# Later value, maxima and transposition transfers, more places for turned terms and remainder rows, and x pairs in middle beats, in a gated attention and feed-forward kernel

## Chip, cores and metric

One core of one Trainium2 chip. The time is the device time of one execution in microseconds (us): the kernel before takes 1727.56 us as the median of 3 runs (1726.11 to 1729.72). TensorE is called PE here, VectorE DVE, ScalarE ACT, GpSimd POOL. SyncE is called SP; its queue issues all the transfers of this kernel.

## The reference, cut to what matters

```
def reference(A_x, A_wq, A_wk, A_wv, A_wo, A_beta, B_x, w_gate, w_up, w_down, gate_w):
    g = sigmoid((x * gate_w).sum(-1, keepdims=True))
    a = A_ref(x, wq, wk, wv, wo, beta)
    b = (silu(x @ w_gate) * (x @ w_up)) @ w_down
    return g * a + (1 - g) * b

    # A_ref: 32 heads of 18, N = 4 segments s of L = 512 rows
    logits = qs @ ks.T * scale + mask          # inside one segment
    a_dot = softmax(logits) @ vs
    a_mem = (phi(qs) @ M) / (phi(qs) @ z + 1e-6)
    o = sigmoid(beta) * a_mem + (1 - sigmoid(beta)) * a_dot
    M, z = M + phi(ks).T @ vs, z + phi(ks).sum(0)
```

x has 2048 rows of 576, w_gate and w_up are 576 x 4608, w_down is 4608 x 576, all float32.

## The kernel before, in words

Three stages follow one another, and the matrix work of all of them is on PE.

**Stage 1** (to about 234 us) makes q, k, v and the memory terms, and leaves them in DRAM for what follows: `stk` and `stw` (stacked queries and keys), `vd` (values), `med` (memory). Its last loop, `for n in range(8)` over units of `v`, also starts what the next stage needs first: raw weights, splits of x and the first remainder rows.

**Stage 2** (234 to about 1640 us) is the feed-forward part, with the attention of all heads woven into it. `seq` lists 72 positions: two halves of the rows (`half`) times 36 column blocks of 128 (`f`). A position makes gate and up of one block for 1024 rows with seven products instead of eight, `seven(bank, j)` for j = 0 to 6. One product is six matmuls (L1392) of 128x512 on split float16 weights `wo__` and x tiles `xo`, and a seventh (L1395) that carries the columns of x that are left over from 512; its weights are the remainder rows `rem`, a tile `rh` that `r_fetch(f)` loads from DRAM (`rc`). There are two such tiles, `rhs[f % 2]`. Between products the position calls `tick()` eight times, k = 0 to 7 (5 and 6 with no product between them), and each tick ends in `beat(k, half)`.

A beat does three things in this order, all of it issued in program order on the engines:

1. it runs the deferred work that is due (`due`, filled by `defer(beats, fn)`): splits of weights, loads, sums, the splits `hh` and `hl` of the hidden block (ACT L1261, DVE L1264);
2. it runs some of the sixteen down-projection groups. They exist in every third position (`q == 0`), cover the three blocks before, and are nine matmuls each (L1161, weights `hh` and `hl`, moving side `dw`). Two banks of PSUM take turns for them, and DVE frees a bank by adding it into `ya` (L1168 the first time, L1170 after that). How many groups a beat gets is in `SHARE`, and for position 3 alone in `FSHARE`, chosen by `early[0]`;
3. it runs attention steps (`next(att)`), by a credit that grows by `TICK`. In the first half steps run only in positions with groups, in beats 2 to 7.

The attention generator `att_gen` counts steps `tau`; five steps are one unit `u` of 4 heads by 512 rows, `n` the step in it. One step touches several units, each at another age: scores for the row maxima (`s_bank`, PE L890, DVE L908), the maxima transposed, stored to DRAM by `m_store` (L982) and read back as an extra row of the queries by `row_load` (L301), then twelve steps after the first the transposed scores with their exponentials (`t_bank`: PE L1001, ACT L1005, POOL L1013), two steps later the float16 split of the terms (DVE L1101 or ACT L1103, POOL L1105) and three steps after that the products with the values (`pv_step`, L1029 and L1031). `v_fetch` loads the values of the next 20 steps from `vd`. In the second half, even units are "turned": exponentials of untransposed scores (L942), split (POOL L947), transposed by DMA (`turn`, L951), then multiplied (`pv_turned`, L963). The parts for turned units sit in `homes`, six places for each name, and `TURN` lists how many steps after `tau` each part runs.

Between the halves stands a break of `BREAK` = 10 beats that runs the last sixteen groups of the first half: beats 0 and 1 are called as ordinary beats, and as `brk[0]` is set there they also run an attention step each; the other eight run two groups each, in four banks.

The first half makes its weight tiles from raw weights (`w_make`: POOL L370, ACT L374, DVE L378) and keeps them in DRAM (`wc`), the second loads them back. `x_second` makes the seven combinations of x for the second half in positions 24 to 35: POOL `total` (L1311), ACT `high` (L1318), DVE `low` (L1321). Its table `steps` gives for each the position after 24 + 6z, the beat, the function and the combination j.

**Stage 3** (from about 1640 us) is the output projection; its weights are split by `c_open` once attention has run out (DVE L1209).

Of the kernel before, what the change touches and what calls it, by code (L numbers as in the profile page):

```python
# [42 lines left out]
TURN = (1, 3, 7, 17)  # L43
# [5 lines left out]
FSHARE = (0, 0, 0, 2, 3, 4, 4, 3)  # L49
# [21 lines left out]
def gated_mix(ctx, tc, xT, xrest, wf, wfr, wfh, wd, wv, wo, beta, cmask, ident, bmask, out):  # L71
# [283 lines left out]
    def r_fetch(f):  # L355
        nc.sync.dma_start(rhs[f % 2][:96].rearrange("p j n -> p (j n)"), rc[f // 4, :, f % 4])
# [38 lines left out]
    with ExitStack() as st:  # L395
# [337 lines left out]
        for s in range(NSEG):  # L733
# [49 lines left out]
            if s == 3:  # L783
# [12 lines left out]
                for z in range(2):  # L796
                    rhs.append(wop.tile([P, 7, P], F16, name=f"rh{z}", bufs=1))
                start = w_make(0)
            for n in range(8):
# [23 lines left out]
                else:  # L823
# [4 lines left out]
                    for k, t, v in ((0, rhs[0][96:], 0.0), (1, kst[0], -1.0), (3, kst[1], -1.0), (6, rhs[1][96:], 0.0)):  # L828
                        if n == k:
                            nc.gpsimd.memset(t, v)  # L830
                    if n == 1:
                        r_fetch(0)
# [11 lines left out]
    with ExitStack() as st:  # L844
# [76 lines left out]
        turned = set()  # L921

        def turn_open(u):
# [5 lines left out]
            for name, ids in (("pq", ((2, 0), (2, 1), (3, 0))), ("pk", ((3, 1), (4, 0), (4, 1)))):  # L929
                homes[name] = []  # L930
                for a, b in ids:
                    t = xo.tile([P, 2, 8 * P], F16, name=f"xo{a}{b}")
                    homes[name] += [t[:, z] for z in range(2)]

        def spot(name, u, n):
            return homes[name][(5 * (u // 2) + n) % 6]
# [113 lines left out]
        def att_gen():  # L1050
            N = 10 * NB
            for tau in range(N + TL + VL + 5):
# [15 lines left out]
                z = tau - TL - VL - 1  # L1068
# [186 lines left out]
        opened, early, brk = [0], [0], [0]  # L1255
# [14 lines left out]
        def beat(k=None, half=0):  # L1270
# [8 lines left out]
            share = (SHARE, FSHARE)[early[0]][k]  # L1279
            for n in range(max(share, 1)):  # L1280
# [4 lines left out]
                credit[0] += TICK[half][busy] * (opened[0] if half else k > 1 or brk[0])  # L1285
# [8 lines left out]
        def x_second(new, z):  # L1294
# [105 lines left out]
        for pos, (half, f) in enumerate(seq):  # L1400
# [68 lines left out]
            early[0] = int(pos == CH)  # L1469
            turn_of[0] = () if pos < 24 else (1, 3)  # L1470
            ops, rem = wops.pop((half, f)), rhs[f % 2]
# [41 lines left out]
            if f == FT - 1:  # L1513
                groups += feed(half, f)
                if half == 0:
                    brk[0] = 1
# [109 lines left out]
```

## Time and profile before

| what | us |
| --- | --- |
| median of 3 runs | 1727.56 |
| the profiled execution's own time | 1725.81 |
| its span, first to last instruction | 1724.1 |
| stage 1, 0 to 234: PE busy | 227.39 |
| second stage, 926 to 1640 (second half): PE busy of 714 | 705.65 |
| stage 3, 1640 to 1724: PE busy | 80.67 |
| DVE busy, whole span | 1347.3 |
| ACT busy, whole span | 1066.3 |
| POOL busy, whole span | 885.6 |

A timeline row reads: start, duration, engine, line, operation, output<-inputs, shape, and in brackets how long the engine sat idle before it and what ended that idle time. A row of waits reads: who waited for whom, then us in total, how often, and the longest. A row of windows gives start and end, the length, and for each engine the busy time with the number of instructions, then the granted PE clock (1.00 is full), the busy share of the DMA engines, and GB/s. A row of the chain of waits gives start, length, and the work or transfer that the end hung on.

### The profile page before, as it was taken

Reading aid. Unit: us, or ns where it says so; the run is one execution under the profiler, and the core shown is the slowest. Engines: PE = TensorE matmul, PEld = TensorE weight load, DVE = VectorE, ACT = ScalarE, POOL = GpSimd, SP = SyncE. Lnnn points to the kernel's source line nnn. Section 1 sums busy time; section 2 is a strip of 40 time slices with the busy share of each in tenths; the row PEclk is TensorE's granted clock in tenths of the full one; section 3 lists DMA queues with packets and bytes.
Section 4 is the critical chain, followed back from the end, with each engine's and each line's share of the span. In section 5 each row is a group of like instructions: output and inputs, shape, how many; then the busy total and the mean of one; then the engine's idle time right before and its main releaser. Section 6 shows DMA issues by size and latency. Waiting matters only on the chain.

```text
span 1724.1 us, 35228 instructions
## 1 busy us (share of the span) xinstructions
PE 1684.5 (98%) x12267; PEld 1093.1 (63%) x12267; DVE 1347.3 (78%) x3286; ACT 1066.3 (62%) x1907; POOL 885.6 (51%) x1187
## 2 busy tenths in 40 slices
PE   9999998999999999999999999999999999999999
PEld 7898865556655665565555556656656655665599
DVE  6687666789888988888886888887878787875555
ACT  6666567677777777766774664665565566464411
POOL 3336552266656665565553755555555555543121
PEclk9999999999999999999999999999999999999999
DMA  8666675665776666536435476786587669653543
GB/s 282 219 229 221 221 257 203 206 210 169 239 229 198 184 220 194 171 112 193 158 124 172 118 173 154 164 196 146 132 203 174 129 166 203 155 122 115 183 142 137
DMA packets 341670, 311.30 MB, mean 181 GB/s; under 512 B 193396, under 2 KB 258676, under 8 KB 341492
## 3 DMA queue, kind: packets, MB, share of 16 engines
q1 hardware_dynamic: 341492, 309.05, 61.8%
q8 instruction: 96, 1.57, 0.4%
q14 instruction: 82, 0.67, 0.1%
HBM read 183.20 MB, written 99.55 MB: 164 GB/s over the span
## 4 chain that ended last, share of the span: by engine, by line
PE 71%; DVE 10%; ACT 9%; issue 3%; DMA 3%; POOL 2%; SPq 1%; DVEq 0%; ACTq 0%; POOLq 0%
PE bank L1392 30%; PE bank L1161 19%; PE bank L224 7%; PE bank L1395 5%; PE bank L890 3%; PE bank L1001 2%; PE bank L1029 1%; ACT L1499 1%; DVE ya L1170 1%; ACT row L1499 1%; ACT pe L1005 1%; PE bank L1031 1%; PE bank L963 1%; DVE junk L908 1%; DMA stw<-q 1%
## 5 line engine op out<-in xcount | busy, mean ns | idle before, releaser
L1161 PE MATMUL bank<-dw,hh 128*128 128x320 f16 (+1 forms) x2304 | 437.9, 287 | 13.8 <-DVE ya L1170 9.5
L1161 PE MATMUL bank<-dw,hl 128*128 128x320 f16 (+1 forms) x1152 | 330.5, 287 | 0.9 <-DVE dw L1141 0.6
L1105 POOL TENSOR_TENSOR p<-pe,p 128x512 f16<-128x512 f32 x220 | 271.7, 1235 | 78.7 <-DVE p L1101 50.2
L1161 PEld LDWEIGHTS <-hh 128*128 128x128 f16 x2304 | 224.9, 98 | 100.9 <-issue 19.9
L1005 ACT ACTIVATE pe<-bank 128x512 f32<-128x512 f32 x220 | 130.1, 591 | 190.6 <-PE bank L1001 181.9
L1170 DVE SCALAR_TENSOR_TENSOR ya<-bank,sc,ya 128x320 f32<-128x320 f32 x352 | 177.2, 511 | 57.2 <-PE bank L1161 55.0
L1395 PE MATMUL bank<-xr,rh 128*128 128x512 f16 x504 | 191.2, 379 | 1.9 <-DMA rh<-rc 1.9
L908 DVE CUSTOM_DVE_ANT_0 junk<-bank,cm 128x128 bf16<-128x128 f32 (+2 forms) x352 | 169.3, 481 | 14.0 <-PE bank L890 7.4
L1013 POOL TENSOR_SCALAR_AFFINE_SELECT pe<-pe 128x256 f32<-128x256 f32 (+1 forms) x220 | 89.5, 407 | 164.6 <-ACT pe L1005 153.0
L1264 DVE SCALAR_TENSOR_TENSOR hl<-hh,row 128x512 f16<-128x512 f16 x144 | 125.2, 870 | 47.8 <-ACT hh L1261 46.7
L1161 PEld LDWEIGHTS <-hl 128*128 128x128 f16 x1152 | 112.7, 98 | 30.2 <-DVE hl L1264 0.6
L890 PE MATMUL bank<-kst,qst 108*128 108x512 bf16 (+3 forms) x512 | 124.8, 299 | 5.9 <-ACT pe L1005 5.2
L1001 PE MATMUL bank<-qst,kst 111*128 111x512 bf16 (+3 forms) x352 | 103.3, 300 | 3.9 <-ACT pe L1005 2.8
L1101 DVE CAST p<-pe 128x512 f16<-128x512 f32 x202 | 106.4, 527 | 0.0
L1497 DVE TENSOR_TENSOR row<-bank,row 128x512 f32<-128x512 f32 x72 | 49.7, 690 | 64.4 <-ACT bank L1496 64.4
L370 POOL TENSOR_TENSOR ws<-raw 128x256 f32<-128x256 f32 x72 | 66.5, 924 | 64.2 <-DMA raw<-in_wf_dram 35.3
L224 PE MATMUL bank<-xo,qhi 128*128 128x512 f32 x288 | 93.0, 403 | 0.5 <-DVE xo L134 0.2
L1261 ACT ACTIVATE hh<-row 128x512 f16<-128x512 f32 x144 | 89.0, 618 | 3.8 <-DVE row L1507 3.8
L467 POOL TENSOR_TENSOR q<-qr,q 128x512 bf16<-128x512 f32 x36 | 47.8, 1328 | 84.3 <-ACT q L466 74.8
L1492 ACT ACTIVATE row<-bank 128x512 f32<-128x512 f32 x72 | 42.9, 596 | 76.4 <-PE bank L1395 76.2
L1395 PEld LDWEIGHTS <-rh 128*128 128x128 f16 x504 | 49.3, 98 | 61.8 <-issue 2.4
L1496 ACT ACTIVATE bank<-bank 128x512 f32<-128x512 f32 x72 | 41.9, 582 | 72.6 <-PE bank L1395 70.7
(1090 smaller groups left out, 4228.3 us busy)
## 6 DMA issues: line engine op xcount, KB each, us to landing
xo<-in_wf_dram SPq DMA_DIRECT2D x65, 320.0 KB
raw<-in_wf_dram SPq DMA_DIRECT2D x72, 256.0 KB
dc<-dw SPq DMA_DIRECT2D x36, 432.0 KB
dw<-dc SPq DMA_DIRECT2D x36, 432.0 KB
rh<-rc SPq DMA_DIRECT2D x72, 168.0 KB
draw<-in_wd_dram SPq DMA_DIRECT2D x36, 288.0 KB
xo<-in_xT_dram SPq DMA_DIRECT2D x33, 256.0 KB
vd<-vps SPq DMA_DIRECT2D x8, 912.0 KB
```

The lines of the kernel that those rows point to most:

```text
L224: nc.tensor.matmul(t, st[n], mv[n], start=(n == 0), stop=(n == 13))
L890: nc.tensor.matmul(t[:, c:c + w], qs[:KR, pr, P * i:P * i + P], ks[:KR, pr, 0:w], start=True, stop=True)
L908: nc.vector.tensor_tensor_reduce(junk.bitcast(BF)[:, :w], t[:, c:c + w], cm[:, L - w:L], 1.0, -3.0e38, OP.add, OP.max, m[:, k:k + 1])
L1001: nc.tensor.matmul(t[:, c:c + w], ks[:KR + 3, pr, P * j:P * j + P], qs[:KR + 3, pr, P * j:L], start=True, stop=True)
L1005: nc.scalar.activation(pe, t, AF.Exp, scale=SCALE)
L1101: nc.vector.tensor_copy(p1, pe)
L1105: nc.gpsimd.tensor_sub(p2, pe, p1)
L1161: nc.tensor.matmul(t, p, d[:, q, cs], start=(f == CH * c and n == 0), stop=(f == CH * c + CH - 1 and n == 2))
L1170: nc.vector.scalar_tensor_tensor(ya[:, i, cs], t, inv[c], ya[:, i, cs], op0=OP.mult, op1=OP.add)
L1264: nc.vector.scalar_tensor_tensor(lo, hi, -STEP, src, op0=OP.mult, op1=OP.add)
L1392: nc.tensor.matmul(t, w[:, p, z], x[z][:, q], start=first and n == 0, stop=False, skip_group_check=True)
L1395: nc.tensor.matmul(t, rem[:, RPOS[j]], XR[j], start=False, stop=True, skip_group_check=True)
```

## The change

The edits, in the order of the program:

- the remainder rows get a third tile: `rhs[f % 3]`. The load for block 1 moves into the last loop of stage 1, and the planned one at position 0 is left out. The third tile's rest is cleared on POOL two beats into stage 2 (one instruction more);
- position 3 takes its groups by `SHARE` like all others; `FSHARE` and `early` are gone;
- `brk` is gone: beats 0 and 1 of the break run no attention steps, so that all attention steps from there on come two later against the positions and beats. There are 340 steps as before;
- in `att_gen`, the maxima are stored and read back one step later in their unit (`m_store` at n = 2, `row_load` at n = 4), the values are fetched five steps later, and the DMA transposition of a turned term one step later (`TURN[2]` 7 to 8). The turned low and high terms `pk` get four more places in a pool of their own (ten in all);
- in `x_second` the sums and splits named in the diff move to beats 4 and 5 from beats 5 to 7.

```diff
-TURN = (1, 3, 7, 17)
+TURN = (1, 3, 8, 17)
-FSHARE = (0, 0, 0, 2, 3, 4, 4, 3)
...
-        nc.sync.dma_start(rhs[f % 2][:96].rearrange("p j n -> p (j n)"), rc[f // 4, :, f % 4])
+        nc.sync.dma_start(rhs[f % 3][:96].rearrange("p j n -> p (j n)"), rc[f // 4, :, f % 4])
...
-                for z in range(2):
+                for z in range(3):
                     rhs.append(wop.tile([P, 7, P], F16, name=f"rh{z}", bufs=1))
...
-                    if n == 1:
-                        r_fetch(0)
+                    if n in (1, 5):
+                        r_fetch(n // 5)
...
+        tp = pool(st, "tp", 1)
...
+            homes["pk"] += [tp.tile([P, 8 * P], F16, name=f"pk{z}") for z in range(4)]
         def spot(name, u, n):
-            return homes[name][(5 * (u // 2) + n) % 6]
+            return homes[name][(5 * (u // 2) + n) % len(homes[name])]
...
-                if n == 1 and 1 <= u <= 2 * NB and u - 1 not in turned:
+                if n == 2 and 1 <= u <= 2 * NB and u - 1 not in turned:
                     m_store(u - 1)
-                if n == 3 and 1 <= u <= 2 * NB and u - 1 not in turned:
+                if n == 4 and 1 <= u <= 2 * NB and u - 1 not in turned:
                     row_load(u - 1)
...
-                z = tau - TL - VL - 1
+                z = tau - TL - VL - 6
                 if z % 20 == 0 and 0 <= z < N and z // 20 + 1 < 4 * NSEG:
                     v_fetch(z // 20 + 1)
...
+        defer(2, lambda: nc.gpsimd.memset(rhs[2][96:], 0.0))
...
-            share = (SHARE, FSHARE)[early[0]][k]
+            share = SHARE[k]
...
-                credit[0] += TICK[half][busy] * (opened[0] if half else k > 1 or brk[0])
+                credit[0] += TICK[half][busy] * (opened[0] if half else k > 1)
...
-                steps += ((0, 3, high, 0), (0, 4, low, 0), (0, 5, total, 1), (0, 5, high, 5), (0, 6, low, 5), (0, 7, total, 4),
+                steps += ((0, 3, high, 0), (0, 4, low, 0), (0, 4, total, 1), (0, 4, high, 5), (0, 5, low, 5), (0, 5, total, 4),
...
-                steps += ((0, 5, high, 0), (0, 6, low, 0), (0, 7, total, 1), (1, 2, high, 5), (1, 3, low, 5), (1, 4, total, 4),
+                steps += ((0, 4, high, 0), (0, 5, low, 0), (0, 5, total, 1), (1, 2, high, 5), (1, 3, low, 5), (1, 4, total, 4),
...
-                plan.append((1 if nxt[1] else 10, lambda f=nxt[1]: r_fetch(f)))
+                if pos:
+                    plan.append((1 if nxt[1] else 10, lambda f=nxt[1]: r_fetch(f)))
...
-            ops, rem = wops.pop((half, f)), rhs[f % 2]
+            ops, rem = wops.pop((half, f)), rhs[f % 3]
```

Three places show how the instructions move. The first is PE in position 3, from the end of its third product (`xr` are the leftover columns of x, `rh` the remainder rows; `hh` are weights of a down group). Before:

```order
L1395 MATMUL bank_3113<-xr_1449,rh_2445 128x512
L1392 LDWEIGHTS wo__3051
L1392 MATMUL bank_3115<-xo_2260,wo__3051 128x512
L1392 LDWEIGHTS wo__3051
L1392 MATMUL bank_3115<-xo_2260,wo__3051 128x512
```

and now:

```order
L1397 MATMUL bank_3118<-xr_1449,rh_2444 128x512
L1162 LDWEIGHTS hh
L1162 MATMUL bank_3181<-dw,hh 128x320
L1162 LDWEIGHTS hh
L1162 MATMUL bank_3181<-dw,hh 128x320
L1162 LDWEIGHTS hl
L1162 MATMUL bank_3181<-dw,hl 128x320
```

Two down groups, 18 matmuls, come before the fourth product instead of after it, two after that product as before, and beats 5 and 6 run one group less each.

The second is PE at the break, from the last product of position 35 (`qst` and `kst` are attention's stacked queries and keys, `p` its terms). Before:

```order
L1395 MATMUL bank_11838<-xr_1756,rh_2445 128x512
L1001 LDWEIGHTS kst_2766
L1001 MATMUL bank_11873<-qst_2768,kst_2766 128x384
L890 LDWEIGHTS qst_2436
L890 MATMUL bank_11875<-kst_2437,qst_2436 128x256
L1001 LDWEIGHTS kst_2766
L1001 MATMUL bank_11873<-qst_2768,kst_2766 128x128
L890 LDWEIGHTS qst_2436
L890 MATMUL bank_11875<-kst_2437,qst_2436 128x256
L1029 LDWEIGHTS p_11461
L1029 MATMUL bank_11898<-v,p_11461 128x57
```

and now:

```order
L1397 MATMUL bank_11842<-xr_1756,rh_2446 128x512
L1162 LDWEIGHTS hh
L1162 MATMUL bank_11884<-dw,hh 128x320
L1162 LDWEIGHTS hh
L1162 MATMUL bank_11884<-dw,hh 128x320
L1162 LDWEIGHTS hl
L1162 MATMUL bank_11884<-dw,hl 128x320
```

Two attention steps went from between the last product and the down groups into the second half.

The third is DVE in position 24, around one `low` of `x_second` (`xo`<-`xo`,`sc`). Before:

```order
L1101 CAST p_9063<-pe 128x512
L378 SCALAR_TENSOR_TENSOR wo__8895<-ws,sc,wo__8895 128x512
L1321 SCALAR_TENSOR_TENSOR xo_8702<-xo_8702,sc 128x512
L1170 SCALAR_TENSOR_TENSOR ya<-bank_9071,sc,ya 128x320
L974 TENSOR_REDUCE acc<-bank_9082 128x152
```

and now:

```order
L377 SCALAR_TENSOR_TENSOR wo__8804<-raw,sc,wo__8804 128x512
L1323 SCALAR_TENSOR_TENSOR xo_8706<-xo_8706,sc 128x512
L1171 SCALAR_TENSOR_TENSOR ya<-bank_8999,sc,ya 128x256
L1171 SCALAR_TENSOR_TENSOR ya<-bank_9010,sc,ya 128x320
L907 ISA junk,mb_2438<-bank_9027,cm 128x128
```

The low stands one beat earlier, behind the split of another pair of weights (L377), and the addition into `ya` that was behind it is now behind a cast and a split alone.

More of the change, by code (lines that the diff above doesn't have):

```diff
@@ L827, in gated_mix @@
                         first_split(6, n)
-                    for k, t, v in ((0, rhs[0][96:], 0.0), (1, kst[0], -1.0), (3, kst[1], -1.0), (6, rhs[1][96:], 0.0)):
+                    for k, t, v in ((0, rhs[0][96:], 0.0), (1, kst[0], -1.0), (3, kst[1], -1.0), (4, rhs[1][96:], 0.0)):
                         if n == k:
                             nc.gpsimd.memset(t, v)
-                    if n == 1:
-                        r_fetch(0)
+                    if n in (1, 5):
+                        r_fetch(n // 5)
                     if n > 2:
@@ L1254, in gated_mix @@
         credit = [-1.0]
-        opened, early, brk = [0], [0], [0]
+        opened = [0]
         later = [False]
@@ L1468, in gated_mix @@
             later[0] = half == 1 and f > 0
-            early[0] = int(pos == CH)
             turn_of[0] = () if pos < 24 else (1, 3)
-            ops, rem = wops.pop((half, f)), rhs[f % 2]
+            ops, rem = wops.pop((half, f)), rhs[f % 3]
             hh = fp.tile([P, 2, L], F16, name="hh")
@@ L1515, in gated_mix @@
                 if half == 0:
-                    brk[0] = 1
                     for n in range(BREAK):
```

## The prediction

> **What bounds the kernel now.** I read the page's busy times first, then the windows by stage, then who waited for whom on PE, then the timeline and the chain of waits at the long stalls.
>
> ```profile
> PE 1684.5 (98%) x12267; PEld 1093.1 (63%) x12267; DVE 1347.3 (78%) x3286; ACT 1066.3 (62%) x1907; POOL 885.6 (51%) x1187
> ```
>
> PE is busy for 98% of the span, and its work is the same before and after. So the change can only win from PE's idle time and from stretches at a lower clock. The windows say where those lie:
>
> ```profile
> 234.00:300.00 66.00, 58.50 (x312) 30.65 (x311) 41.05 (x93) 48.79 (x91) 20.63 (x33) 0.97 0.68 235
> 825.00:926.00 101.00, 97.53 (x686) 58.55 (x684) 84.59 (x170) 66.63 (x113) 48.20 (x53) 0.98 0.45 152
> 926.00:1640.00 714.00, 705.65 (x5723) 424.28 (x5722) 550.89 (x1476) 408.31 (x681) 378.23 (x498) 1.00 0.64 159
> 280.00:290.00 10.00, 6.46 (x34) 3.68 (x33) 4.57 (x13) 6.75 (x14) 0.00 (x0) 0.83 0.98 375
> 905.00:915.00 10.00, 9.32 (x61) 6.62 (x61) 7.18 (x19) 4.30 (x8) 7.04 (x7) 0.83 0.60 206
> ```
>
> The first five positions and the break hold the only two places in the feed-forward stage with a clock of 0.83; one such window of ten costs 10 x 0.17 = 1.7 us of matmul progress. The second half has 714.00 - 705.65 = 8.35 us of idle time in 714, in small pieces. The waits on PE:
>
> ```profile
> PE bank L1161 <- DVE ya L1170: 9.5, 16, 1.6
> PE bank L890 <- ACT pe L1005: 5.2, 11, 0.8
> PE bank L1161 <- DVE ya L1168: 3.8, 3, 2.8
> PE bank L1001 <- ACT pe L1005: 2.8, 1, 2.8
> PE bank L1395 <- DMA rh<-rc: 1.9, 1, 1.9
> PE bank L1001 <- DMA wo__12361<-wc: 1.1, 1, 1.1
> ```
>
> These six rows are 24.3 us, and the change touches the owner of each: places, order, or step.
>
> **Part A, remainder rows.** Position 1 waits for its remainder rows, which were issued in position 0 behind other transfers:
>
> ```profile
> 242.83 4.62 DMA rh<-rc
> 247.59 0.38 PE L1395 MATMUL bank<-xr,rh 128*128 128x512 f16 x1 [1.93 <-DMA rh<-rc]
> 253.00 0.72 POOL L370 TENSOR_TENSOR ws<-raw 128x256 f32<-128x256 f32 x1 [7.34 <-DMA raw<-in_wf_dram]
> ```
>
> The third tile lets this load go out in stage 1, so the 1.93 us stall has no cause left. The one POOL clear that is added (two beats into stage 2) falls into the 7.34 us in which POOL sat waiting. That same row is also what can eat the gain: the next weights are made from raw data that lands at 253.00 whenever PE arrives, so a PE that is 1.93 us early may wait for weights instead. Bounds 0 and 1.93; I take the middle, 1.0.
>
> **Part B, position 3.**
>
> ```profile
> 273.25 1.46 PE L1392 MATMUL bank<-xo,wo__3051 128*128 128x512 f16 x6
> 276.79 0.30 PE L1161 MATMUL bank<-dw,hl 128*128 128x320 f16 x1 [0.59 <-DVE dw L1141]
> 281.98 0.38 PE L1161 MATMUL bank<-dw,hh 128*128 128x256 f16 x2 [0.74 <-DVE ya L1168]
> 276.77 6.58 DMA xo<-in_wf_dram
> 285.93 0.69 PE L1161 MATMUL bank<-dw,hh 128*128 128x320 f16 x2 [2.80 <-DVE ya L1168]
> 303.66 2.21 PE bank L1161 x18
> ```
>
> Here 0.59 + 0.74 + 2.80 = 4.13 us are idle, and behind the 2.80 the clock falls (the window at 280), another 1.7. The cause of the 2.80 is a chain: a transfer lands 6.58 us after its issue, ACT waits for it, DVE behind ACT, and the eviction of a down bank behind that, so PE has nothing it may do. Now two groups (2.21 us for 18 matmuls) stand ahead of the fourth product. That work sits earlier, and what PE still owes at 285.93 is 2.21 less. Against it: the earlier pair starts at 273.25 and reaches its last factor 14 matmuls later, 273.25 + 14 x 2.21/18 = 274.97, while that factor is only there at 276.79. So 1.82 us of stall stand where 0.59 stood, 1.23 more, before later stalls shrink by it. What comes out: if the transfer's chain still decides at 285.93, the PE work after it is 2.21 shorter and the clock loss may stay; that is 2.2. If the 2.80 goes with its clock loss, 2.80 + 1.7 - 1.23 = 3.3, and with the 0.74 and the rest of the 0.59 it could be 4.4. If the stall at the front drops the clock instead, a loss of 1.6. I take 2.5, nearer the first; bounds -1.6 and 4.4.
>
> **Part C, x pairs.** Twice a down group waits 1.58 us because the split of an x pair stands ahead of the addition into `ya`:
>
> ```profile
> 690.90 0.55 DVE L1170 SCALAR_TENSOR_TENSOR ya<-bank,sc,ya 128x320 f32<-128x320 f32 x1 [0.39 <-PE bank L1161]
> 696.83 1.65 DVE L1321 SCALAR_TENSOR_TENSOR xo<-xo,sc 128x512 f16<-128x512 f32 x1
> 698.99 0.43 PE L1161 MATMUL bank<-dw,hh 128*128 128x320 f16 x2 [1.58 <-DVE ya L1170]
> 815.23 0.43 PE L1161 MATMUL bank<-dw,hh 128*128 128x320 f16 x2 [1.58 <-DVE ya L1170]
> 683.92 0.74 DVE L1321 SCALAR_TENSOR_TENSOR xo<-xo,sc 128x512 f16<-128x512 f32 x1
> 693.25 0.27 PE L890 MATMUL bank<-kst,qst 108*128 108x256 bf16 x1 [0.81 <-ACT pe L1005]
> 521.21 0.27 PE L890 MATMUL bank<-kst,qst 108*128 108x256 bf16 x1 [0.40 <-ACT pe L1005]
> ```
>
> The split goes one beat earlier, to where DVE had 0.39 us of room. With the shorter of its two durations, 0.74, it makes 0.74 - 0.39 = 0.35 of new stall; with the longer, 1.65, 1.26. So each place gives 0.3 to 1.2. The ACT half of the pair moves too, and with it goes 0.81 - 0.40 = 0.4 at most at the two scores that wait 0.81. I take 2 x 1.23 for DVE, since the long duration stood beside POOL's own sums, which move away too, and 2 x 0.17 for ACT: 2.8. Bounds: 0 (the stall only moves) and 2 x 1.58 + 2 x 0.4 = 4.0.
>
> **Part D, the break.**
>
> ```profile
> 901.25 0.33 PE L1001 MATMUL bank<-qst,kst 111*128 111x384 bf16 x1
> 903.09 0.63 ACT L1261 ACTIVATE hh<-row 128x512 f16<-128x512 f32 x1 [1.55 <-DVE row L1507]
> 903.74 1.28 ACT L1005 ACT_TABLE_LOAD   x1
> 903.85 0.69 DVE L1264 SCALAR_TENSOR_TENSOR hl<-hh,row 128x512 f16<-128x512 f16 x1
> 905.68 0.22 PE L1001 MATMUL bank<-qst,kst 111*128 111x128 bf16 x1 [2.79 <-ACT pe L1005]
> 906.43 19.31 PE bank L1161 x144
> ```
>
> From 901.25 to the end of the sixteen groups is 906.43 + 19.31 - 901.25 = 24.49 us. Eight pairs at full clock take 8 x 2.21 = 17.7, and 19.31 were taken; the 1.6 between is the window of 0.83. In the change the groups start at once. Their first 12 matmuls (1.5 us) need the two older blocks, the next three need `hh` and `hl` of block 35, there at 903.72 and 904.54: by then PE has done 14 of its 144, so 904.54 - 901.25 - 14 x 0.123 = 1.6 us of stall, say 1.8 with the pieces, too short in the row above (1.93) to drop the clock. The two attention steps are paid later: from 901.25 to the stall's start at 905.68 - 2.79 = 902.89, 1.65, and from 905.68 to 906.43, 0.75, together 2.4. So 17.7 + 1.8 + 2.4 = 21.9, gain 2.6. Lower bound 1.0 (the clock falls all the same, 1.6), upper 24.49 - 17.7 - 2.4 = 4.4 (no stall).
>
> [...]
>
> **Part E, later transfers and shifted steps.** Two attention steps move into the second half, and every one there stands elsewhere against DVE's work. What is taken off is SP, which stands in order behind loads that wait for places:
>
> ```profile
> SPq L306 <- PE bank L890: 84.2, 9, 13.5
> ```
>
> `v_fetch` (L306) blocked SP for 84.2 us in nine calls because the last reader of its buffer ran only one step before. Now it comes six steps after, and the row loads, weights and transposes queued behind it are issued sooner. This is worth PE time only where PE waits for a transfer, and in the second half that is the one row of 1.1. Nearly all of the second half's 8.35 us of idle time waits for DVE's additions or ACT's exponentials, which two steps shuffle without taking work away. I take +0.5; the bounds are the other rows of the waits: -3 (four more stalls of about 0.8) and +4 (half the idle time).
>
> **Part F, the tail.** The last weight splits come one beat later:
>
> ```profile
> 1632.20 2.43 DVE L1209 TENSOR_TENSOR wo<-raw,wo 128x480 fp32r<-128x480 f32 x2
> ```
>
> Behind these 2.43 us DVE makes the last `hl`, which the last groups need. Bounds -1.5 and 0; I take -0.2. The four new places of `pk` and the later transposes cost nothing I can find: no matmul of a turned unit stands among the waits above.
>
> **The sum.** 1.0 + 2.5 + 2.8 + 2.6 + 0.5 - 0.2 = 9.2 us. Against the profiled execution's own 1725.81 that is 1716.6. The runs' median, 1727.56, lies 1.75 above that execution; so the runs should show 1718.35, rounded to 1718.
>
> **The rivals.**
>
> R1, the shuffle gives the gain back: ten stalls of 0.8, as the scores at 693.25 show one, in a second half that has 714 us with DVE busy for 550.89 of them. 1725.8 - 9.2 + 8 = 1724.6, with 1.75 about 1726.4. For it: a step table is a fit of DVE's and ACT's order, and this one shifts. Against it: the gains of A to D lie ahead of the second half, and the number of operations stays.
>
> R2, the row of maxima comes late, slower than before. In the first half the row load stands now behind four loads of queries and keys:
>
> ```profile
> 520.63 0.77 SPq L301 DMA_DIRECT2D qst<-mxd  x1
> 523.62 0.74 SPq L1067 DMA_DIRECT2D kst<-stk  x1
> 529.53 0.38 PE L1001 MATMUL bank<-qst,kst 111*128 111x512 bf16 x1
> 1058.59 1.64 DMA qst<-stk
> ```
>
> Before, 529.53 - 520.63 = 8.9 us lay between issue and use; now 529.53 - (523.62 + 0.74) = 5.2. Landings on the chain run from 1.64 to 4.62 and 6.58 us. Above 5.2 it decides: at 6.58 each short cycle loses 1.4, and about ten units of the first half are short, 14 us, so 1725.8 - 9.2 + 14 + 1.75 = 1732.4. For it: SP issues one transfer after another, and a single late one stops the scores and all that is behind them on PE. Against it: the two longest landings were of 168 KB or more, in windows with DMA at its busiest, and the maxima are 6 KB, nearer to the 1.64.
>
> R3, the stalls of B and C only move: DVE has no room in beat 5 (C 0), position 3 still hangs on the transfer (B 1.0 left), the start hangs on raw weights (A 0), and only the break (2.6) and E (0.5) remain. 1725.8 - 4.1 + 1.75 = 1723.5.
>
> R4, the stalls shrink but both places keep their clock of 0.83, because something else than a stall of 2.8 lowers it. Then B gives its 2.2 and D its 1.0: 1725.8 - 9.2 + 0.3 + 1.6 + 1.75 = 1720.3. For it: two cases are few. Against it: in both the low stretch begins right where the stall ends, and the windows without such a stall, the 714 us of the second half, read 1.00.
>
> That the change does what it says is plain from the order of the instructions, so no rival is made of that.
>
> **How the numbers follow.** Forecast 0.56, R3 0.16, R4 0.06, R1 0.11, R2 0.11. A measurement of this kernel tells about 0.2%, 3.5 us, from no change: faster is below 1724.1, slower above 1731.0. Forecast, R3 and R4 are faster, 0.78; R1 is the same, 0.11; R2 slower, 0.11. The forecast's own range, with A to E at about half of their bounds together, is 1713 to 1722. The whole range reaches over R3 and R1 and leaves out R2 and a tail below: 1712 to 1728.
>
> **What would show it.** A: no wait for `rh<-rc` at the first remainder matmul of position 1, and the same instant for the weights of position 2. B: the window of ten around position 3 at clock 1.00, one stall of some 1.8 at its first group, none of 2.8. C: no 1.58 for `ya` in positions 24 and 30, and less than 0.5 one beat before. D: the groups of the break right behind position 35, 19.5 us long, clock 1.00. E: SP's wait at the value load near zero; PE's idle time in the second half 8 us, give or take 3. R2 would show as scores waiting for `qst<-mxd`; R1 as more rows of 0.6 to 0.9 for `ya` or `pe` after the break. A clock of 0.83 in a new place makes the forecast wrong by 1.7 each, and row loads that land late make it wrong altogether.

## The result, and the profile after

The changed kernel takes 1723.37 us, the median of 9 runs (1721.72 to 1725.13), against 1729.72 of 9 runs of the kernel before (1726.11 to 1732.3): a ratio of 0.9966 [0.9956, 0.9976], some 5.9 us. The prediction said 1718, with 1712 to 1728 around it. The two profiled executions lie closer together, 1725.81 and 1723.37, 2.4 us, as the one of the kernel before lies 3.9 us below the median of its runs; the experiments come back to that.

Line numbers of the changed kernel are up to two off the old ones (L1161 is L1162, L1170 is L1171, L1508 is L1510); those of an experiment can be off by some more. The page's busy times, and windows of the stages and places shown before:

```profile
PE 1683.8 (98%) x12267; PEld 1092.6 (63%) x12267; DVE 1351.8 (79%) x3287; ACT 1066.1 (62%) x1906; POOL 885.8 (51%) x1188
```

```profile
234.00:300.00 66.00, 60.65 (x335) 32.36 (x334) 43.90 (x98) 48.93 (x93) 20.68 (x33) 1.00 0.69 238
926.00:1640.00 714.00, 704.47 (x5769) 426.20 (x5768) 556.21 (x1492) 409.57 (x683) 381.62 (x502) 1.00 0.65 158
280.00:290.00 10.00, 9.91 (x71) 6.71 (x70) 6.03 (x18) 8.26 (x17) 0.31 (x1) 1.00 0.96 363
900.00:910.00 10.00, 7.00 (x43) 4.78 (x44) 7.29 (x11) 3.10 (x5) 3.18 (x3) 0.83 0.63 202
```

The window around position 3 is now nearly full in this profile, 9.91 of 10 us at clock 1.00 where it was 6.46 at 0.83; in four other profiles with the same share of groups the clock still fell there (see position 3 below). The break is not mended: there the clock is 0.83 as before, and PE is idle for 3 us of 10. The waits on PE of the changed kernel:

```profile
PE bank L1162 <- DVE ya L1171: 8.0, 17, 0.9
PE bank L1162 <- DVE hl L1266: 3.1, 2, 2.1
PE bank L889 <- ACT pe L1006: 3.0, 8, 0.4
PE bank L1162 <- DVE ya L1169: 1.9, 2, 1.0
PE bank L889 <- DMA kst<-stk: 1.4, 2, 1.1
PE bank L1162 <- ACT hh L1263: 1.1, 2, 0.9
```

The long waits are gone: no 1.93 for `rh<-rc`, no 2.80 for the first additions into `ya`, none of 1.58 for the later ones, no 0.81 for `pe`. New are 2.1 us for `hl` (at the break) and 1.4 us for keys, `kst<-stk`. SP no longer waits in front of the value load at all, where it had 84.2 us.

Where PE's time went is best seen by position. Each number is the length of a stretch in a profiled execution, taken from the start of the first remainder matmul (`xr`,`rh`) of a position to that of a later one; "35" holds the break, and the last column runs from position 70 to the end of the span.

| run | 0-2 | 3 | 6-15 | 24 + 30 | 35 | 36-69 | 70-end | profiled us |
| --- | --- | --- | --- | --- | --- | --- | --- | --- |
| before | 34.83 | 38.02 | 205.41 | 76.18 | 35.52 | 687.00 | 110.22 | 1725.81 |
| after | 34.30 | 34.97 | 208.07 | 73.73 | 33.82 | 688.48 | 110.93 | 1723.37 |
| e1 before again | 34.11 | 39.09 | 205.68 | 75.87 | 35.52 | 686.69 | 109.76 | 1725.47 |
| e11 before, third | 34.77 | 36.73 | 205.89 | 75.87 | 35.53 | 689.20 | 109.68 | 1726.83 |
| e2 values back | 34.35 | 36.93 | 206.61 | 73.47 | 33.18 | 688.41 | 110.81 | 1722.71 |
| e3 late sums | 33.96 | 36.92 | 205.87 | 74.32 | 32.15 | 688.49 | 110.74 | 1721.21 |
| e4 break steps | 34.09 | 36.40 | 207.92 | 73.86 | 35.53 | 687.69 | 109.69 | 1723.71 |
| e5 gated sums | 34.28 | 35.25 | 207.55 | 73.20 | 30.44 | 688.65 | 110.57 | 1719.33 |
| e6 values, maxima back | 34.49 | 36.41 | 206.66 | 73.41 | 34.93 | 688.56 | 110.59 | 1724.56 |
| e7 share of 3 back | 33.69 | 38.77 | 206.05 | 73.89 | 32.12 | 688.48 | 110.82 | 1722.88 |
| e8 pairs back | 34.65 | 34.96 | 207.37 | 77.16 | 33.86 | 688.46 | 110.72 | 1725.66 |
| e9 values between | 35.57 | 35.99 | 206.70 | 73.32 | 30.44 | 688.21 | 110.87 | 1720.34 |
| e10 turn back | 34.56 | 35.91 | 206.24 | 73.96 | 30.44 | 688.41 | 110.93 | 1719.63 |
| e12 earlier tail | 34.24 | 35.34 | 206.44 | 73.10 | 30.44 | 690.48 | 109.64 | 1718.26 |

The first two rows account for the 2.4 us: position 3 gives 3.05, positions 24 and 30 give 2.45, the break 1.70, the start 0.28 (0.53, less a stage 1 that ended 0.25 later); positions 6 to 15 take back 2.66, the second half 1.48, the end 0.71, position 27 another 0.24. The 3.05 of position 3 holds a low clock that the first of the two executions met there and the second did not.

### The profile page after: what moved, and what is told of

Its sections match the earlier page's. It is cut to its first block, busy times and chain, and to the rows that moved or that the text cites. A ratio compares the mean times of both kernels' runs of the same rounds, so it can differ in the third digit from the quotient of the medians.

```text
span 1721.7 us, 35261 instructions
## 1 busy us (share of the span) xinstructions
PE 1683.8 (98%) x12267; PEld 1092.6 (63%) x12267; DVE 1351.8 (79%) x3287; ACT 1066.1 (62%) x1906; POOL 885.8 (51%) x1188
## 4 chain that ended last, share of the span: by engine, by line
PE 73%; DVE 11%; ACT 7%; issue 3%; DMA 3%; SPq 1%; POOL 1%; DVEq 0%; ACTq 0%; POOLq 0%
PE bank L1394 32%; PE bank L1162 18%; PE bank L223 8%; PE bank L1397 5%; PE bank L889 3%; PE bank L1002 2%; PE bank L1030 1%; DVE ya L1171 1%; ACT L1501 1%; PE bank L1032 1%; PE bank L964 1%; DVE junk L907 1%; DVE p L1102 1%; DMA xo<-in_wf_dram 1%; ACT row L1501 1%
## 5 line engine op out<-in xcount | busy, mean ns | idle before, releaser
L1162 PE MATMUL bank<-dw,hh 128*128 128x320 f16 (+1 forms) x2304 | 436.9, 286 | 12.8 <-DVE ya L1171 8.0
L1162 PE MATMUL bank<-dw,hl 128*128 128x320 f16 (+1 forms) x1152 | 329.8, 286 | 3.7 <-DVE hl L1266 3.1
L1162 PEld LDWEIGHTS <-hh 128*128 128x128 f16 x2304 | 224.7, 98 | 99.5 <-issue 17.6
L1171 DVE SCALAR_TENSOR_TENSOR ya<-bank,sc,ya 128x320 f32<-128x320 f32 x352 | 176.8, 511 | 57.6 <-PE bank L1162 55.4
L1266 DVE SCALAR_TENSOR_TENSOR hl<-hh,row 128x512 f16<-128x512 f16 x144 | 129.1, 897 | 45.3 <-ACT hh L1263 44.4
L1162 PEld LDWEIGHTS <-hl 128*128 128x128 f16 x1152 | 112.5, 98 | 34.1 <-DVE hl L1266 3.8
L1509 DVE SCALAR_TENSOR_TENSOR row<-bank,sc,row 128x512 f32<-128x512 f32 x72 | 53.9, 749 | 41.7 <-PE bank L1397 21.2
```

What stands on the lines that cost most here:

```text
L1162: nc.tensor.matmul(t, p, d[:, q, cs], start=(f == CH * c and n == 0), stop=(f == CH * c + CH - 1 and n == 2))
L1171: nc.vector.scalar_tensor_tensor(ya[:, i, cs], t, inv[c], ya[:, i, cs], op0=OP.mult, op1=OP.add)
L1266: nc.vector.scalar_tensor_tensor(lo, hi, -STEP, src, op0=OP.mult, op1=OP.add)
```

## The experiments

### The break (e3, e4, e5)

At the break of the changed kernel the groups start at once, as the order said. Then PE waits, on DVE:

```profile
898.68 0.82 DVE L1140 SCALAR_TENSOR_TENSOR dw<-draw,sc,dw 128x576 f16<-128x576 f32 x1 [1.10 <-ACT dw L1139]
899.68 2.94 POOL L1349 TENSOR_TENSOR raw<-raw 128x512 f32<-128x512 f32 x2 [14.35 <-DMA raw<-in_xr_dram]
900.08 1.42 DVE L1510 SCALAR_TENSOR_TENSOR row<-row,sc 128x512 f32<-128x512 f32 x1
901.42 1.37 DVE L1142 TENSOR_SCALAR dw<-dw 128x576 f16<-128x576 f16 x1
902.71 1.28 DVE L1266 SCALAR_TENSOR_TENSOR hl<-hh,row 128x512 f16<-128x512 f16 x2
903.45 0.45 PE L1162 MATMUL bank<-dw,hl 128*128 128x320 f16 x1 [2.12 <-DVE hl L1266]
```

In the kernel before:

```profile
902.98 0.74 DVE L1508 SCALAR_TENSOR_TENSOR row<-row,sc 128x512 f32<-128x512 f32 x1
903.63 0.30 DVE L1141 TENSOR_SCALAR dw<-dw 128x576 f16<-128x576 f16 x1
910.10 2.61 POOL L1347 TENSOR_TENSOR raw<-raw 128x512 f32<-128x512 f32 x2
```

There the two DVE operations ahead of `hl` took 0.74 and 0.30 us; here 1.42 and 1.37. What is new beside them is POOL's sums for the remainder rows of x, which ran from 899.68 to 902.62. Before, an attention step stood ahead of them on POOL, and they ran from 910.10, after the splits.

e4 puts the two steps back:

```diff
...
-                credit[0] += TICK[half][busy] * (opened[0] if half else k > 1)
+                credit[0] += TICK[half][busy] * (opened[0] if half else k > 1 or brk[0])
...
+                    brk[0] = 1
```

> The changed kernel with the two attention steps put back into beats 0 and 1 of the break. Theory: the break is 1.7 longer, as in the kernel before, and the second half 2.4 shorter by the two steps, so that leaving them out was worth nothing: 1722.7, plus or minus 2 for the shifted second half. POOL's sums stand behind the attention's own work and DVE's 16-bit scaling takes 0.30. Rival, the prediction's part D: the steps in the break cost 2.6, time 1726.0.

It measured 1723.94 us (ratio to before 0.997 [0.9958, 0.9981]), and the same by position: the break back at 35.53, 1.71 longer; the second half 0.79 shorter; the end 1.24 shorter. What the missing steps gave at the break was lost behind it.

e3 tried to move POOL's sums by issuing their load later, in beat 7 instead of beat 4:

```diff
-... (4, load, 1), (11, high, 5), ...
+... (7, load, 1), (11, high, 5), ...
```

> The changed kernel with the second load of remainder rows of x three beats later (from beat 4 to beat 7 of position 35), so that POOL's two sums run after the split of the last hidden block and not beside it. Theory: beside POOL's sums DVE took 1.42 instead of 0.74 and 1.37 instead of 0.30 us, which made hl of block 35 late, PE idle for 2.12 and the clock fall to 0.83; now these take 0.74 and 0.30, the stalls before the break's second block are 1.4 together instead of 3.0, the clock stays at 1.00, and position 35 with the break is 33.82 - 3.2 = 30.6 us; near 1720.2. Rival: the stall is owed to DVE's order alone and position 35 stays within 0.4 of 33.8; time 1723.4.

The edit failed as an experiment: SP stood at an earlier transfer anyway, the sums ran at 899.30, and DVE's two operations took 1.39 and 1.37. It stands as a second measurement of nearly the same kernel (1722.09 us, ratio 0.996 [0.9947, 0.9972]), and it showed something else. The stall at `hl` was the same, the clock behind it not. The four us behind the stall, as a row of windows, in the changed kernel:

```profile
902.00:906.00 4.00, 2.55 (x11) 1.56 (x12) 2.97 (x5) 2.00 (x4) 0.62 (x1) 0.68 0.57 181
```

And e3, its stall in the timeline and the same window:

```profile
903.06 0.31 PE L1162 MATMUL bank<-dw,hl 128*128 128x320 f16 x1 [2.08 <-DVE hl L1266]
```

```profile
902.00:906.00 4.00, 2.94 (x24) 2.37 (x25) 3.07 (x7) 1.62 (x3) 0.24 (x1) 1.00 0.67 221
```

Over the six profiles without the gate of e5 and without the steps, this stall was 1.85 to 2.17 us; the clock fell behind it in four and held in two (e3 and e7, with position 35 at 32.1).

The traces show in what the two cases differ. A low stretch of this stage lasted 3.41 us at a clock of 0.50 (6.83 in e6), so it cost some 1.7 us (an estimate, half its length), and within one trace the low stretches start whole multiples of 3.413 us apart: in the kernel before at 285.81, 907.04 and 1722.82, which is 182 and 239 of them. Counted from there, each trace can be divided into windows of that length, and they lie elsewhere in each execution (one starts at 899.99 in the changed kernel, at 897.86 in e3). Here are the window that holds the stall and the one behind it, in the changed kernel:

```profile
899.99:903.41 3.42, 0.45 (x2) 0.11 (x2) 3.42 (x5) 2.50 (x5) 2.55 (x2) 1.00 0.00 0
903.41:906.82 3.41, 3.37 (x14) 2.03 (x15) 1.56 (x3) 0.59 (x1) 0.00 (x0) 0.50 0.95 306
```

In e3 the idle time is divided between two windows, and the clock stays:

```profile
897.86:901.27 3.41, 2.23 (x16) 1.22 (x14) 2.94 (x4) 1.19 (x3) 1.89 (x2) 1.00 0.23 80
901.27:904.68 3.41, 1.62 (x13) 1.25 (x14) 3.19 (x5) 2.35 (x4) 0.97 (x1) 1.00 0.41 129
904.68:908.09 3.41, 3.41 (x31) 2.79 (x30) 2.33 (x4) 0.00 (x0) 0.74 (x1) 1.00 0.98 300
```

In the fourteen traces, 15 windows of stage 2 stand right before a low stretch; PE was busy for 0.13 to 0.45 of each. Of the 5736 other windows at full clock only one has less than 0.47: 0.44, from 244.85 in the kernel before. So in these runs the clock went with how much PE idled inside one such window, and one and the same pair of stalls had a low clock behind it (0.89 and 2.12 in the changed kernel) or had none (0.89 and 2.08 in e3), by where the windows happened to lie.

e5 holds the sums back by their data: one more POOL instruction ahead of them reads the last `hl` (`mk` is a new tile of one column for its result).

```diff
...
+                if j == 1:
+                    t = hs[0, FT - 1][1][:, 1, 0:1]
+                    nc.gpsimd.tensor_sub(mk, t, t)
                 nc.gpsimd.tensor_sub(o, p, q)
```

> The changed kernel with one tiny POOL instruction ahead of the break's sums that reads the last hl, so that POOL's sums cannot run before DVE has made it (later loads, tried before, did not move them: they ran at 899.30). Theory: without POOL beside it DVE takes 0.74 and 0.30 us again for the two operations ahead of hl, hl of block 35 is there 1.7 us sooner, the stall at it falls from 2.1 to 0.4, and the clock has no reason to fall: position 35 with the break 30.5 us, against 33.82 (clock 0.83) and 32.15 (clock 1.00); time 1723.4 - 2.5 = 1721. Rival: DVE's durations are its own (1.4 and 1.37 stay) and position 35 is 32 to 34 as before.

The same rows in e5:

```profile
899.56 0.74 DVE L1514 SCALAR_TENSOR_TENSOR row<-row,sc 128x512 f32<-128x512 f32 x1
900.22 0.30 DVE L1143 TENSOR_SCALAR dw<-dw 128x576 f16<-128x576 f16 x1
901.18 0.31 PE L1163 MATMUL bank<-dw,hl 128*128 128x320 f16 x1 [0.37 <-DVE hl L1267]
901.80 0.19 POOL L1352 TENSOR_TENSOR mk<-hl 128x1 f32<-128x1 f16 x1 [16.99 <-DVE hl L1267]
901.95 2.62 POOL L1353 TENSOR_TENSOR raw<-raw 128x512 f32<-128x512 f32 x2
903.08 0.55 DVE L1172 SCALAR_TENSOR_TENSOR ya<-bank,sc,ya 128x320 f32<-128x320 f32 x1 [0.50 <-PE bank L1163]
```

The expectation came step by step: 0.74 and 0.30, a stall of 0.37, clock 1.00, position 35 at 30.44. The time is 1719.33 us, 0.9946 [0.9933, 0.9959] of before, where 1721 was expected; with e9 and e10 it is the fastest version. The break now takes what the prediction worked out for it, 35.52 - 30.44 = 5.08 less than before.

### The value load, the maxima and positions 6 to 15 (e2, e6, e9)

```diff
-                z = tau - TL - VL - 6
+                z = tau - TL - VL - 1
```

> The changed kernel with the value fetch where it was before the change (five steps earlier). Theory: in positions 9 and 15 the 456 KB value load makes SP wait (1.9 us for v<-vd), so the key loads behind it are late and PE waits for them (1.09 and 0.32); without it both positions go back to 35.6 us, 1.25 + 1.00 = 2.25 less, and SP's waits in front of the value load come back (about 84 us) at no price: near 1721. Rival, as the prediction's part E has it: the free SP is worth something in the second half, and undoing it costs 0.5 to 4 there: 1722 to 1726.

e2 took 1721.29 us (0.9957 [0.9944, 0.9969]). In position 9 of the changed kernel SP waits for the value load before it issues a store, and the key loads behind that come too late:

```profile
SPq L348 <- DMA v<-vd: 1.9, 1, 1.9
```

```profile
411.14 0.38 PE L889 MATMUL bank<-kst,qst 108*128 108x512 bf16 x1 [1.09 <-DMA kst<-stk]
```

In e2 position 9 is 35.63 again. SP's waits in front of the value load came back, 76.1 us in 11 pieces, and the second half is 688.41 against 688.48: the SP time that the change sets free is worth nothing there. But position 6, where the load now falls again, rose to 35.39 from 34.63 before the change.

e6 puts the maxima back too:

```diff
-                z = tau - TL - VL - 6
+                z = tau - TL - VL - 1
...
-                if n == 2 and 1 <= u <= 2 * NB and u - 1 not in turned:
+                if n == 1 and 1 <= u <= 2 * NB and u - 1 not in turned:
                     m_store(u - 1)
-                if n == 4 and 1 <= u <= 2 * NB and u - 1 not in turned:
+                if n == 3 and 1 <= u <= 2 * NB and u - 1 not in turned:
                     row_load(u - 1)
```

> The changed kernel with the value fetch and the storing and reading of the maxima both as before the change. Theory: the two are what lengthens positions 6, 9 and 15, since both put something ahead of the key loads on SP (108.5, 106.4 and 108.3 together in three runs with both, 107.1 with the maxima alone, 105.9 and 106.2 before the change): now 105.9 to 106.2, no wait of PE for kst<-stk. Second half within 0.5 of 699. Time near 1721.3. Rival: the lengthening is owed to the earlier start of these positions against the transfers, and they stay at 107 or more.

1723.22 us (0.9965 [0.9952, 0.9979]). Positions 9 and 15 were 35.64 and 35.68, as the theory said, but position 6 was 35.84 with a new wait for keys, 107.16 for the three together: the theory holds only in part. The row of waits of SP there names a landing, not PE:

```profile
SPq L348 <- DMA xo<-in_wf_dram: 0.9, 1, 0.9
```

The key load that PE waited for was issued at 353.15 in e6, and at 353.11 in the kernel before, although PE arrived 1.35 us earlier. That points at transfers that set the pace of this stretch, whoever stands ahead on SP.

e9 takes e5 and sets the value load between the two places:

```diff
-                z = tau - TL - VL - 6
+                z = tau - TL - VL - 3
```

> The kernel of e5 (sums held back) with the value fetch three steps earlier than in the change, in the step behind a unit's key loads and not in the one ahead of them. Theory: SP then has no value load to wait for ahead of the key loads of positions 9 and 15, these go to 35.7 and 35.9 (36.06 and 36.95 in e5), and the load now issued late in position 6 leaves that at 34.7 to 35.1: 1.5 us less than e5, 1717.8. Rival: the whole stretch up to position 16 hangs on transfers, since position 16 began between 532.2 and 534.5 in ten runs whether position 6 began at 324.8 or 328.8; then position 16 begins at 533 again and the time stays at 1719.3.

1719.27 us (0.9958 [0.9945, 0.997]): the rival came. Position 9 was 35.63, position 15 36.12, and position 16 began at 534.26, though position 6 began at 327.56. Over all kernels with the new share in position 3, position 6 began at 324.8 to 327.6, up to 4 us before the old kernel's 327.7 to 328.8; position 16 began at 531.6 to 534.3, against 533.6 to 534.5. Their means differ by 2.1 us at position 6 and by 0.9 at position 16. Which transfer holds this stretch back, no run singled out.

### Position 3 and the x pairs (e7, e8)

e7 brings back the old share in position 3:

```diff
...
-            share = SHARE[k]
+            share = (SHARE, FSHARE)[early[0]][k]
```

> The changed kernel with the old share of groups in position 3. Theory (part B): position 3 is 38.0 to 39.1 us again, as in two runs of the kernel before, instead of 35.0 to 36.9 in four runs with the new share; time up by 2.2 to 1725.6. Rival: the shorter position 3 comes from the earlier remainder rows and loads, and it stays under 37.

e8 brings back the old beats of the x pairs:

```diff
-... (0, 4, total, 1), (0, 4, high, 5), (0, 5, low, 5), (0, 5, total, 4), ...
+... (0, 5, total, 1), (0, 5, high, 5), (0, 6, low, 5), (0, 7, total, 4), ...
...
-steps += ((0, 4, high, 0), (0, 5, low, 0), (0, 5, total, 1), ...
+steps += ((0, 5, high, 0), (0, 6, low, 0), (0, 7, total, 1), ...
```

> The changed kernel with the old beats of the x pairs. Theory (part C): positions 24 and 30 are 38.3 to 38.5 and 37.6 to 37.7 us as in two runs of the kernel before, instead of 36.8 to 37.8 and 36.5 to 36.7; the wait of 1.58 for ya is back in both; time up by 2.2 to 1725.6. Rival: the later value fetch freed DVE or POOL there, and the positions stay as in the change.

The waits on PE in the timeline, of e7 in position 3 and then of e8 in positions 24 and 30:

```profile
282.36 0.38 PE L1163 MATMUL bank<-dw,hh 128*128 128x256 f16 x2 [1.58 <-DVE ya L1170]
285.99 0.69 PE L1163 MATMUL bank<-dw,hh 128*128 128x320 f16 x2 [2.50 <-DVE ya L1170]
```

```profile
698.05 0.43 PE L1162 MATMUL bank<-dw,hh 128*128 128x320 f16 x2 [1.58 <-DVE ya L1171]
814.81 0.43 PE L1162 MATMUL bank<-dw,hh 128*128 128x320 f16 x2 [1.58 <-DVE ya L1171]
```

In e7 the long stalls of position 3 return, with a length of 38.77; the time is 1725.0 us (0.9982 [0.9972, 0.9991]). In e8 the two waits of 1.58 return to the hundredth, positions 24 and 30 take 77.16, and the time is 1725.57 us (0.9984 [0.9975, 0.9992]). Each edit alone carries its term.

What position 3 gains depends on the clock as well. At its front all ten profiles with the new share have stalls of 1.14 and 0.59 us (1.14 and 1.1 in e2 and e3). Behind them the clock fell in four (e2, e3, e4, e6: position 3 took 36.40 to 36.93 us) and held in six (34.96 to 35.99). In the changed kernel the two stalls lie in two windows, in e4 in one; the first two rows are the changed kernel's:

```profile
271.94:275.35 3.41, 2.31 (x13) 1.04 (x12) 1.20 (x2) 3.40 (x8) 0.00 (x0) 1.00 1.02 345
275.35:278.76 3.41, 2.55 (x17) 1.61 (x17) 3.41 (x10) 1.66 (x5) 1.87 (x2) 1.00 1.02 377
272.91:276.32 3.41, 1.45 (x10) 0.61 (x9) 2.73 (x6) 2.71 (x7) 0.74 (x1) 1.00 1.00 339
276.32:279.74 3.42, 3.42 (x14) 1.76 (x12) 2.35 (x7) 1.66 (x4) 1.36 (x2) 0.50 1.00 370
```

With the old share the clock fell there in three of four (38.02, 39.09 and e7's 38.77) and held in e11 (36.73).

### Transposition and places, and the end (e10, e12)

e10 is e5 with the old transposition and six places:

```diff
-TURN = (1, 3, 8, 17)
+TURN = (1, 3, 7, 17)
...
-            homes["pk"] += [tp.tile([P, 8 * P], F16, name=f"pk{z}") for z in range(4)]
```

> The kernel of e5 with the transposition one step earlier and the six places as before the change. Theory: no PE wait named a transposition before or after, so the second half (position 36 to 71) stays at 699.2 within 0.3 and the time at 1719.3. Rival: the later transposition costs something in the second half, where the change with the break's steps put back (e4) took 698.26 against 697.3 and 697.6 before the change: then 0.7 to 1.0 less, 1718.5.

1719.63 us (0.9959 [0.9946, 0.9973]), second half 688.41 against 688.65: no difference, for the two edits together. e12 is e5 with attention a little faster in the second half:

```diff
-TICK = ((0.0, 1.0), (0.76, 1.0))
+TICK = ((0.0, 1.0), (0.77, 1.0))
```

> The kernel of e5 with attention steps in the second half taken a little faster (0.77 of a step per beat without groups instead of 0.76), so that they end where they did before the change and the output weights' splits stand one beat earlier again. Theory (part F): from position 70 to the end took 110.6 to 110.9 us in nine runs with the steps two later, and 109.7 to 110.2 in four runs with the old place; here it takes 109.7 to 110.2. The stretch from position 36 to 70, 688.65 in e5, moves by an unknown amount within 2 either way as every step there moves; the time is 1718.4, plus or minus 2. Rival: the tail is bound elsewhere and stays at 110.6 or more.

The stretch from 70 to the end took 109.64, as expected; the second half 690.48, 1.83 more; 1720.45 us in all (0.9956 [0.9942, 0.997]), no gain over e5. What the end loses in the changed kernel is once more a wait for `hl`, beside POOL:

```profile
1631.62 1.40 POOL L1231 TENSOR_TENSOR o<-o,me 128x576 f32<-128x576 f32 x1 [6.20 <-DMA me<-med]
1631.75 1.82 DVE L1510 SCALAR_TENSOR_TENSOR row<-row,sc 128x512 f32<-128x512 f32 x1
1634.27 0.31 PE L1162 MATMUL bank<-dw,hl 128*128 128x320 f16 x1 [1.02 <-DVE hl L1266]
```

Before the change the same POOL operation met the weight split that took 2.43 us (1.22 in the changed kernel, at 1629.26 and without POOL), ahead of this chain; with the steps two later it meets the chain itself. In e12 L1514 (the same operation) took 0.74 again.

### The kernel before, twice more (e1, e11)

> The kernel before, unchanged, for a second profile. Its profiled execution took 1725.81 us, while its nine runs have a median of 1729.72. Theory: one place that hangs on a transfer (position 3, or a load in the second half) is some 4 us longer in a usual run, so a second profile near 1729 shows one position 2 to 4 us longer than in the first. Rival: the 4 us are spread thinly (the clock, or all positions by 0.05), and no position differs by over 0.5.

> The kernel before once more, for a third profile. Two profiled executions took 1725.81 and 1725.47, while its timed runs have a median of 1728.4 and spread over 8 us. Theory: position 3 (38.02 and 39.09) and positions 24 and 30 vary with landings and with the clock, so one of these or position 35 differs by over 1 us if this execution takes 1728 or more. Rival: the difference is spread.

e1 had a median of 1728.06 us over 10 runs, e11 one run of 1726.83. Position 3 took 36.73 to 39.09 in three profiles of the kernel before. The shortest is e11's, where the clock held although its three stalls (1.11, 1.53 and 1.80) are together longer than the first profile's (0.59, 0.74 and 2.80). In e11 the second half is 2.2 to 2.5 us longer than in the other two. Two thirds of that stand in position 42, which took 36.36 instead of 34.92 and 34.61, with this wait (a score waits; the row names `hl`, which a score does not read, and SP issued loads of `kst` at 1031.13 and 1032.44, so a transfer as the cause is a guess that no run tested):

```profile
1034.41 0.38 PE L890 MATMUL bank<-kst,qst 108*128 108x512 bf16 x1 [1.41 <-DVE hl L1264]
```

In all nine runs of the change and its variants with the shifted steps at their new places, position 42 took 35.31 to 35.33 us, and the second half 688.2 to 688.7. A second half that varies less would be one reason why the medians differ by more (5.9) than the profiled pair (2.4); which edit steadies position 42 is open.

No profile of the kernel before was taken in an execution of 1729 us or more, so e1's theory of one long position was not tested. The granted clocks of its timed runs say where part of the time goes: of 66 on record with the experiments, the seven at 0.999 or more took 1724.9 us on the mean, the 30 at 0.998 1727.2, and the 29 at 0.997 or less 1729.6. A clock lower by 0.001 over the span is one low stretch of 3.41 us more, 1.7 us by its length. The mean clock is 0.9976 for these and 0.9982 for the nine runs of the change, so about 1 us of the 5.9 is fewer low stretches (an estimate from these figures).

## Why the prediction was right, and where it was not

The direction and the range held; the sum was 9.2 us and the gain 5.9 by the runs, 2.4 by the profiled pair. The forecast's own range, 1713 to 1722, was missed by 1.4. That the time agrees with the 1723.5 of rival R3 (the stalls of B and C only move) is chance: B and C came nearly whole, and the shortfall is at the break and in positions 6 to 15. Step by step:

- **A, remainder rows, 1.0:** 0.5 over positions 0 to 2. The stall of 1.93 is gone, and positions 1 and 2 are 1.4 longer, by waits on ACT of 0.53 and 0.27 among others. On the mean of three old and eleven new profiles the gain is 0.2. Right in kind, near the lower bound; no run put the two tiles back alone.
- **B, position 3, 2.5:** 3.05 in the pair, and 38.0 to 35.9 (2.0) on the mean of three old and ten new runs; the new front stall was 1.14 + 0.59 against the 1.8 worked out. Right, and e7 shows the cause. The size in the pair owes something to luck: the clock fell in the first of the two and held in the second. The branch that the prediction priced at 1.6, a front stall that itself drops the clock, came in four of ten profiles. What the prediction lacked is what follows: it added the gain to the end, while the stretch to position 15 hangs on landings and gives 1.3 of it back on the same mean (205.7 to 206.9). Rival R2 had the mechanism, a load queued too late behind others on SP, but named the maxima; it was the keys.
- **C, x pairs, 2.8:** 2.45 in the pair, 2.3 on the mean. Right, and e8 shows it. The row that made the difference, 1.65 us for a split that elsewhere took 0.74, stood beside a POOL operation from 696.40 to 697.93. The prediction took that for POOL's sums; it is attention's split of the terms, and the split of x got away from it (first row before, second row after):

```profile
696.40 1.53 POOL L1105 TENSOR_TENSOR p<-pe,p 128x512 f16<-128x512 f32 x1 [1.34 <-PE bank L890]
689.36 0.75 DVE L1323 SCALAR_TENSOR_TENSOR xo<-xo,sc 128x512 f16<-128x512 f32 x1
```

- **D, the break, 2.6 (5.0 there, 2.4 paid later):** this step failed. The break gave 1.70. The prediction put DVE's durations of before (0.74, 0.30) into a place where POOL now ran beside DVE, and so worked out a stall of 1.8, "too short" to lower the clock; it was 0.89 + 2.12, and the clock fell. The length of one stall was also the wrong measure for the clock: 0.89 + 2.08 in e3 left it at 1.00. Part D did not ask what the two steps had held back: on POOL they stood ahead of the sums. With that undone (e5) the break takes what D had, 5.08 less.
- **E, shifted steps and freed SP, +0.5 beside the 2.4 paid:** the second half is 1.48 longer, not 1.9. The free SP is worth nothing (e2), nor are the later transposition and the new places (e10).
- **F, the end, -0.2:** -0.71 in the pair, 1.0 on the mean (109.8 to 110.8), well inside the bounds; e4 and e12 show that it is the place of the steps.

The term that was mis-sized most is D, by 3.3 us at the break; the one that was missing is the 2.66 given back in positions 6 to 15. Rival R4, low clocks that stay for another reason, did not come: every low stretch of this stage stands behind a window with PE busy for 0.13 to 0.45 of it, and where the break's stall went (e5, e9, e10, e12), the clock was 1.00. At the break of the kernel before, the low stretch did not begin right where the stall ended, as the case against R4 had it, but 1.36 us later (905.68 and 907.04). R1 and R2 did not come either: the second half is 1.48 longer, not 8, and no wait names `qst<-mxd`.

## What to carry to other kernels

Before an instruction is taken away from one engine, look at what stood behind it on the others: here the two attention steps had kept POOL's sums and DVE's chain to `hl` apart, and side by side two DVE operations took 1.42 and 1.37 us instead of 0.74 and 0.30. Where a stretch is paced by landings, compare the start of a later position, not the length of the one that was mended: here position 6 began 2.1 us earlier on the mean, position 16 only 0.9. And one profile does not tell what a stall costs: here one of 2.12 us at the break was followed by a low stretch, some 1.7 us more, and one of 2.08 by none, by how the idle time lay in the windows of 3.41 us. So compare several profiles, or the granted clocks of many runs.

## What the runs showed of the hardware

- DVE beside POOL: in the changed kernel `row` from `row` and `sc` (L1510), 0.74 us in the kernel before, took 1.42 at the break and 1.82 at the end, and the 16-bit scaling of `dw` (L1142) 1.37 instead of 0.30. In e5, where POOL's sums came later, both were at 0.74 and 0.30 again. The additions into `ya`, which read one input from PSUM, took 0.55 us beside POOL's sums of 2.62 (903.08 in e5) and 0.55 with POOL idle (906.97 in the changed kernel). Why some of DVE's operations took longer beside POOL and these did not, no run singled out.
- The clock fell in four of six runs behind one and the same pair of stalls (0.89, then 1.85 to 2.17 us, with 0.45 of work between) and held in two. In fourteen traces it fell behind windows of 3.413 us in which PE was busy for 0.13 to 0.45, and, but for one window at 0.44, not behind those with 0.47 or more. These shares are as exact as the modelled ends of the matmuls; what sets the clock beyond that, no run showed.
